# Attention scores in fp32 with one head in each half of the array's rows, in a fused attention and soft-MoE kernel

## The chip, the cores and the metric

One core of one Trainium2 chip runs the whole program. The metric is the device time of one execution in microseconds (us); the time before is the median of three runs, 644.68 us (644.61 to 645.15).

## The reference

Three layers follow each other. Sparse attention over 4 batches and 8 heads, 576 tokens, head size 64:

```python
scores = scale * np.matmul(q, k.transpose(0, 1, 3, 2))
thresh = np.max(scores, axis=-1, keepdims=True) - tau
scores = np.where(scores >= thresh, scores, -1000000000.0)
attn = np.exp(scores - np.max(scores, axis=-1, keepdims=True))
attn = attn / (np.sum(attn, axis=-1, keepdims=True) + 1e-09)
out = np.matmul(attn, v)
```

Then a soft mixture of 8 experts (`d.T @ x` into 32 slots, two layers `w1`, `w2` per expert, and back to 2304 tokens), and a feed-forward layer with weights `w_in` (512 x 2048) and `w_out` with a sigmoid gate. All inputs and outputs are fp32.

## The kernel before

**Stages.** `attention()` runs 16 units; a unit is two heads of one batch. Each unit has nine tiles of 128 query rows by 576 keys: four chunks times two heads (t = 0 to 7), and a tile t = 8 that holds the last 64 rows of both heads. `experts()` follows, then `ffn()`.

**The loop.** In `attention()` one loop (L887) runs over all 144 tiles; iteration i issues `scores(i)` (TensorE), `row_max(i-1)` (VectorE, out of PSUM), `exps(i-1)` (ScalarE), `trans(i-4)` (TensorE transposes of the weights `p`), `mask(i-2)` (VectorE). Product steps `attn_v` (weights times values, tile `o_ps`) run at set offsets of a unit (L932 to L937), and the next unit's q and k are transposed by `prep_rest` and `prep_main` (L939 to L945). From i = 5 the engines keep the order in which the program issues their work (L889); the loads on the queue of SP are not held to it. Scores lie in a pool `ps_s` of two PSUM buffers of two banks each, one buffer for a tile.

**Scores by halves.** `prep_main` transposes q and k of both heads at once; ScalarE copies the result to fp32r (the high half), VectorE takes the difference (the low half, `split`, L328), and DMAs from SP's queue (L397) stack high and low halves of one head on top of each other in `a_st`, `b_st`, `kl0`, `kl1`: 8 moves a unit. With that, one fp32r matmul of 128 rows sums two products, and a tile takes four (L452):

```python
for half in range(2):
    for j, (lh, rh, m) in enumerate(prods):
        te.matmul(ps[0:m, half, 0:HS], lh, rh[:, half * HS:(half + 1) * HS], ...)
```

A tile t = 8 takes eight. `first_unit` (L802) makes the same operands for unit 0 without DMAs, from transposes of each head twice.

**Weights.** Expert weights come in quarters of 0.5 MB into rings. Ring `a` holds 12 quarters; ring `b` takes the place of a pool that frees at i = 126; rings `c` to `k` take freed places near the end of attention (L1002 to L1018). 42 of 64 quarters are held when `experts()` starts; the other 22 are loaded as layer 1 has read `a` and `b` (L1060), and layer 2 `c` and `d` (L1102). SP's queue issues all loads.

Of the kernel before, what the change touches and what calls it, by code (L numbers as in the profile page):

```python
# [19 lines left out]
def kernel(  # L20
# [14 lines left out]
    nc = tc.nc  # L35
# [43 lines left out]
    order = [(1, e) for e in range(4)] + [(2, 0), (2, 1)] + [(1, e) for e in range(4, E)]  # L79
# [28 lines left out]
    def add_ring(name, n, side=LEFT, spread=False):  # L108
        ring_ctx[name] = ctx if name in "bk" else ExitStack()
        rings[name] = ring_ctx[name].enter_context(  # L110
            tc.tile_pool(name="ring_" + name, bufs=1, side=side)
        )
        if n:
            load_quarters(name, n, spread)

# [94 lines left out]
    def late_piece(pool, j, wl):  # L210
        n, kc = divmod(j, KC)
        cols = slice(n * DM, (n + 1) * DM)
        return decoding(
            pool, ("late", j), DM,
            lambda top, rest: po.tensor_add(out=wl[:, kc, cols], in0=top, in1=rest),
        )
# [18 lines left out]
    def attention():  # L235
# [22 lines left out]
        pr = pool(loads, "pr", 1, RIGHT)  # L258
# [7 lines left out]
        b_st = []  # L266
        for i in range(2):
            t = stk[i].tile([P, 2 * R + C * P], F32R, name=f"b_st{i}")
            ve.memset(t[:, 0:R].bitcast(F32), 0.0)
            b_st.append(t)  # L270
# [7 lines left out]
        nat, rest, hl, stacks, vt = {}, {}, {}, {}, {}  # L278
# [40 lines left out]
        def halves(u, nm):  # L319

            if u not in hl:
                hl[u] = {
                    "q": pr.tile([P, 2, S], F32R, tag="q", name="q_hl"),
                    "k": pr.tile([P, 2, S + R], F32R, tag="k", name="k_hl"),
                }
            return hl[u][nm]

        def split(nm, src, hi, lo):  # L328

            if nm == "q":  # L330
                ac.activation(out=hi, in_=src, func=AF.Copy, scale=neg)
                return lambda: ve.scalar_tensor_tensor(
                    out=lo, in0=src, scalar=neg, in1=hi.bitcast(F32),
                    op0=ALU.mult, op1=ALU.subtract,
                )
            ac.copy(out=hi, in_=src)
            return lambda: ve.tensor_sub(out=lo, in0=src, in1=hi.bitcast(F32))

        def prep_rest(u, bank):


# [9 lines left out]
            def after():  # L351
                x = halves(u, "q")
                lows = [split("q", t[:, 0, :], x[:, 0, 0:R], x[:, 1, 0:R])]
                ends = halves(u, "k").rearrange("p a (e n) -> p a e n", n=R)[:, :, 0::S // R, :]
                both = t[:, 1:2, :].to_broadcast([P, 2, R])
                lows.append(split("k", both, ends[:, 0], ends[:, 1]))
                return lambda: [f() for f in lows] and None
# [3 lines left out]
        def prep_main(u, nm, bank):  # L361
# [6 lines left out]
            lo, hi = slice(0, D), slice(D, P)  # L368

            def after():  # L370
                x = halves(u, nm)
                low = split(
                    nm, t.rearrange("p c t -> p (c t)"), x[:, 0, R:S], x[:, 1, R:S]
                )
                return lambda: stack(low)

            def stack(low):
                low()
                x = hl[u][nm].bitcast(F32)
                if nm == "q":  # L380
                    a_st = stk[u % 2].tile([P, S], F32R, tag="a_st", name="a_st")
                    bs = b_st[u % 2]
                    moves = (
                        (a_st[lo, :], x[lo, 0, :]), (a_st[hi, :], x[lo, 1, :]),
                        (bs[hi, R:], x[hi, 0, :]), (bs[lo, R:], x[hi, 1, :]),
                    )
                    stacks[u] = [a_st, bs]
                else:
                    kl0 = stk[u % 2].tile([P, 2, S], F32R, tag="kl0", name="kl0")
                    kl1 = stk[u % 2].tile([P, 2, S + R], F32R, tag="kl1", name="kl1")  # L390
                    moves = [
                        (dst[half], x[src, :, c0:])
                        for dst, src, c0 in ((kl0, lo, R), (kl1, hi, 0)) for half in (lo, hi)
                    ]
                    stacks[u] += [kl0, kl1]
                    hl.pop(u)
                for dst, src in moves:  # L397
                    nc.sync.dma_start(out=dst.bitcast(F32), in_=src)
# [37 lines left out]
        def kl_planes(t):  # L436
            return t[:, 0, :], t[:, 1, :]

        def scores(i):
            u, t = divmod(i, TPU)  # L440
            a_st, bs, kl0, kl1 = stacks[u]
            ps = ps_s.tile([P, 2, 512], F32, tag="s", name="s_ps")


            if t < 2 * C:
                c, h = divmod(t, 2)
                cols = slice((1 + h) * R + c * P, (1 + h) * R + (c + 1) * P)
                prods = [((a_st, bs)[h][:, cols], x[:, 0:S], P) for x in kl_planes((kl0, kl1)[h])]
            else:
                prods = [(bs[:, 0:2 * R], x[:, R:], P) for x in kl_planes(kl1)]  # L450
                prods[1:1] = [(a_st[:, 0:R], x, R) for x in kl_planes(kl0)]
            for half in range(2):  # L452
                for j, (lh, rh, m) in enumerate(prods):
                    te.matmul(
                        ps[0:m, half, 0:HS], lh, rh[:, half * HS:(half + 1) * HS],
                        start=(j == 0), stop=(j == len(prods) - 1),
                    )
            s_ps[i] = ps
# [343 lines left out]
        def first_unit():  # L802


            def both(nm, h):

                if h == 0:
                    t = ps_s.tile([P, 2, 512], F32, tag="s", name="first_t")
                    return t[:, 0, :].rearrange("p (c t) -> p c t", c=C), t[:, 1, 0:R]
                if nm == "q":  # L810
                    return (
                        ps_t.tile([P, C, P], F32, tag="t", name="first_t"),
                        spare(0, [P, R], "first_t"),
                    )
                return bank_m([P, C, P], "first_t"), bank_o([P, R], "first_t")

            wide = {
                nm: stk[0].tile([P, n], F32R, tag=nm, name=nm)
                for nm, n in (("a_st", S), ("kl0", 2 * S), ("kl1", 2 * (S + R)))
            }  # L820
            a_st, kl0, kl1 = wide.values()
            kl0, kl1 = (x.rearrange("p (a n) -> p a n", a=2) for x in (kl0, kl1))
            stacks[0] = [a_st, b_st[0], kl0, kl1]
            k0, l0, k1, l1 = *kl_planes(kl0), *kl_planes(kl1)
            halves = (slice(0, D), slice(D, P))

            def twice(out, rows):
                for half in halves:
                    te.matmul(
                        out[half], rows, ident[0:rows.shape[0], 0:rows.shape[0]],  # L830
                        start=True, stop=True,
                    )

            for nm, h in (("q", 0), ("k", 0), ("q", 1), ("k", 1)):
                main, left = both(nm, h)
                for c in range(C):
                    twice(main[:, c, :], nat[0][nm][:, c, h, :])
                twice(left, rest[0][nm][:, h, :])
                main = main.rearrange("p c t -> p (c t)")
                if nm == "q":  # L840

                    dst = b_st[0][:, R:] if h else a_st
                    low = halves[1 - h]
                    ac.copy(out=dst[:, R:], in_=main)
                    ac.copy(out=dst[:, 0:R], in_=left)
                    for part, src in ((dst[low, R:], main), (dst[low, 0:R], left)):
                        ve.tensor_sub(out=part, in0=src[low, :], in1=part.bitcast(F32))
                else:
                    dst, low, c0 = (k1, l1, R) if h else (k0, l0, 0)
                    ac.copy(out=dst[:, c0:c0 + C * P], in_=main)  # L850
                    ac.copy(out=dst[:, c0 + C * P:c0 + S], in_=left)
                    if h:
                        ac.copy(out=dst[:, 0:R], in_=left)
                    ve.tensor_sub(
                        out=low[:, c0:c0 + C * P], in0=main,
                        in1=dst[:, c0:c0 + C * P].bitcast(F32),
                    )
# [20 lines left out]
        for _ in range(NRA):  # L878
            load_quarters("a", 4, spread=True)
# [518 lines left out]
```

## Time and profile before

| | us |
|---|---|
| median of three runs | 644.68 |
| the profiled execution | 644.8 |
| its span, first to last instruction | 643.0 |
| PE busy / share of the span | 615.1 / 96% |
| DVE busy / share | 428.7 / 67% |
| ACT busy / share | 372.6 / 58% |
| POOL busy / share | 150.9 / 23% |

PE is TensorE, DVE VectorE, ACT ScalarE, POOL GpSimd, SP the engine whose queue issues the DMAs. Ends of matmuls are modelled and overlap, so a stretch of PE is measured from the start of one group to the start of the next. A fp32 matmul shows as two records, a fp32r matmul and a transpose as one. Attention takes the span up to about 360 us, the experts up to about 402, the feed-forward layer the rest.

### The profile page before, as it was taken

What the parts mean: (1) busy time and instruction counts of PE and PEld (TensorE: products, weight loads), DVE (VectorE), ACT (ScalarE), POOL (GpSimd) and SP (SyncE); (2) the same over time, 40 slices, a digit from 0 to 9 for tenths busy, and PEclk for the clock granted to TensorE, in tenths of its full rate; (3) what the DMA queues carried; (4) which work ended last, traced back from release to release, by engine and by line L of the source; (5) the groups of instructions that cost most, each with busy time, mean ns of one, the idle gap of its engine ahead of it and who ended that gap; (6) DMA issues with size and microseconds to landing.
All of it is one profiled execution on the core that took longest, in us unless ns stands there. A gap on an engine that the chain in (4) does not pass through costs nothing.

```text
span 643.0 us, 11172 instructions
## 1 busy us (share of the span) xinstructions
PE 615.1 (96%) x3848; PEld 450.3 (70%) x3848; DVE 428.7 (67%) x1090; ACT 372.6 (58%) x777; POOL 150.9 (23%) x309
## 2 busy tenths in 40 slices
PE   7799999999999999999999899899998999999996
PEld 6667777677776777766776543577776888888884
DVE  5699888898987898978883242999994212242422
ACT  3588777778876787876773010767565353434340
POOL 1263535335352354533441010001100000000000
PEclk9899999999999999999999799999998999999999
DMA  7785676756786577755679899223320000020203
GB/s 198 208 203 127 167 178 182 183 165 161 204 211 172 165 181 183 184 133 156 177 262 333 307 386 378 101 99 131 131 98 1 0 2 0 1 98 1 99 0 98
DMA packets 78568, 97.52 MB, mean 152 GB/s; under 512 B 44592, under 2 KB 48688, under 8 KB 78512
## 3 DMA queue, kind: packets, MB, share of 16 engines
q1 hardware_dynamic: 78512, 96.82, 51.4%
q8 instruction: 30, 0.49, 0.3%
q14 instruction: 26, 0.21, 0.1%
HBM read 64.55 MB, written 4.72 MB: 108 GB/s over the span
## 4 chain that ended last, share of the span: by engine, by line
PE 82%; DMA 6%; DVE 5%; ACT 2%; SPq 2%; issue 1%; ACTq 0%; DVEq 0%
PE s_ps L132 15%; PE o_ps L132 14%; PE y_ps L1289 10%; PE y_ps L1291 10%; PE y_ps L1290 9%; PE pt_ps L132 9%; PE r_ps L132 5%; PE h_ps L1263 2%; DMA w_b<-in_moe_w_dram 2%; DMA raw<-in_moe_w_out_dram 2%; PE acc L1054 2%; PE k_t L132 1%; PE q_t L132 1%; DMA qn<-in_q_dram 1%; DVE p L132 1%
## 5 line engine op out<-in xcount | busy, mean ns | idle before, releaser
L132 ACT ACTIVATE e_sb<-p,mn 128x576 f32<-128x576 f32 x144 | 112.5, 781 | 13.7 <-DVE p L132 12.4
L132 DVE TENSOR_SCALAR_CACHE_REDUCE p<-s_ps 128x576 f32<-128x576 f32 x135 | 101.3, 750 | 26.3 <-PE s_ps L132 19.0
L132 DVE SCALAR_TENSOR_TENSOR p<-p,th,e_sb 128x576 f32<-128x576 f32 x144 | 117.7, 818 | 1.5 <-ACT e_sb L132 1.3
L1289 PE MATMUL y_ps<-wo_h,gh 128*128 128x512 f32 x288 | 114.6, 398 | 0.4 <-ACT gh L1250 0.4
L1290 PE MATMUL y_ps<-wo_l,gh 128*128 128x512 f32 x288 | 113.9, 396 | 0.0
L1291 PE MATMUL y_ps<-wo_h,gw 128*128 128x512 f32 x288 | 113.5, 397 | 0.0
L1252 DVE TENSOR_TENSOR gw<-sg,gh 128x768 fp32r<-128x768 f32 (+2 forms) x49 | 47.0, 962 | 95.1 <-ACT gh L1250 95.1
L132 ACT COPY pt<-pt_ps 128x512 f32<-128x512 f32 x142 | 82.8, 583 | 46.4 <-PE o_ps L132 23.2
L132 POOL TENSOR_TENSOR th<-mn,few 128x1 f32<-128x1 f32 x144 | 64.0, 444 | 180.8 <-DVE p L132 177.5
L1268 ACT ACTIVATE sg<-h_ps 128x512 f32<-128x512 f32 (+1 forms) x96 | 42.4, 489 | 88.3 <-PE h_ps L1263 87.9
L132 PE MATMUL pt_ps<-ident,p 128*128 128x128 f32 x580 | 86.9, 273 | 0.0
L132 PE MATMUL o_ps<-pt,vn 128*64 128x320 f32 (+1 forms) x512 | 85.5, 427 | 0.0
L132 PEld LDWEIGHTS pt_ps<-ident,p 128*128 128x128 f32 x580 | 71.1, 141 | 0.7 <-issue 0.4
L132 PE MATMUL s_ps<-kl,b_st 128*128 128x288 f32 x320 | 68.8, 321 | 1.8 <-DMA kn<-in_k_dram 1.2
L132 PE MATMUL s_ps<-kl,a_st 128*128 128x288 f32 (+1 forms) x320 | 65.7, 318 | 0.7 <-DVE y L132 0.7
L1289 PEld LDWEIGHTS y_ps<-wo_h,gh 128*128 128x128 f32 x288 | 54.3, 189 | 14.3 <-ACT gh L1250 1.1
L132 PEld LDWEIGHTS s_ps<-kl,a_st 128*128 128x128 f32 (+1 forms) x320 | 45.1, 179 | 26.5 <-DVE p L132 9.2
L1291 PEld LDWEIGHTS y_ps<-wo_h,gw 128*128 128x128 f32 x288 | 54.1, 188 | 13.3
L1290 PEld LDWEIGHTS y_ps<-wo_l,gh 128*128 128x128 f32 x288 | 54.3, 189 | 11.4 <-DVE gw L1252 0.2
L132 PEld LDWEIGHTS s_ps<-kl,b_st 128*128 128x128 f32 x320 | 47.8, 191 | 16.5 <-DVE p L132 8.7
L132 PEld LDWEIGHTS o_ps<-pt,vn 128*64 128x64 f32 x512 | 27.3, 135 | 28.3 <-issue 24.7
L1250 ACT CAST gh<-sg 128x768 fp32r<-128x768 f32 (+2 forms) x49 | 40.2, 823 | 1.2
(200 smaller groups left out, 796.3 us busy)
## 6 DMA issues: line engine op xcount, KB each, us to landing
kl<-k_hl SPq DMA_DIRECT2D x30, 320.0 KB, 5.6
kl<-k_hl SPq DMA_DIRECT2D x30, 288.0 KB, 4.2
raw<-in_moe_w_out_dram SPq DMA_DIRECT2D x16, 512.0 KB, 3.3
raw<-in_moe_w_in_dram SPq DMA_DIRECT2D x24, 256.0 KB, 3.4
w_a<-in_moe_w_dram SPq DMA_DIRECT2D x12, 512.0 KB, 4.5
w_a<-in_moe_w_dram SPq DMA_DIRECT2D x6, 1024.0 KB, 10.4
a_st<-q_hl SPq DMA_DIRECT2D x30, 144.0 KB, 2.7
b_st<-q_hl SPq DMA_DIRECT2D x30, 144.0 KB, 2.7
```

What stands on the lines that cost most here:

```text
L132: ins = call(*args, **kw)
L1054: nc.tensor.matmul(acc1[j][kc * NS:(kc + 1) * NS, :], s_in[kc // 2][:, kc % 2, e * NS:(e + 1) * NS], w_rows[1, e, kc][:, j * 512:(j + 1) * ...
L1250: nc.scalar.copy(out=gh[:, a], in_=sg[:, a])
L1252: nc.vector.tensor_sub(out=gw[:, a], in0=sg[:, a], in1=gh[:, a].bitcast(F32))
L1263: nc.tensor.matmul(ps, ws[:, f * P:(f + 1) * P], cs[:, t:t + n, :].rearrange("p t n -> p (t n)"), start=True, stop=True,)
L1268: nc.scalar.activation(out=part, in_=ps, func=AF.Gelu_apprx_sigmoid)
L1289: nc.tensor.matmul(ys[t], gh[:, tk], w_h, start=first, stop=False)
L1290: nc.tensor.matmul(ys[t], gh[:, tk], w_l, start=False, stop=False)
L1291: nc.tensor.matmul(ys[t], gw[:, tk], w_h, start=False, stop=last)
```

## The change

Scores are made from plain fp32 q and k as they come out of the transposes: head 0 in partitions 0 to 63, head 1 in 64 to 127. A matmul contracts over 64 rows of the array; the two heads of a chunk go to two tiles of `ps_s` in turn (both buffers at once), and the tile t = 8 becomes one matmul per head and half, each with its own 64 columns of the array, into one PSUM tile. The splitting, the stacking moves, `b_st` and the pool `pr` go. Scores are issued in even iterations for two tiles, behind `trans`; the product steps and the preparation move to other iterations. A ring `m` holds four quarters from units 10 and 11 on and stays; rings `d` and `e` are halved, and after layer 2 has read it `m` is loaded again; in the feed-forward layer its place holds a partial sum and half of `wl`. The experts are loaded in another order.

```diff
-    order = [(1, e) for e in range(4)] + [(2, 0), (2, 1)] + [(1, e) for e in range(4, E)]
+    order = [(1, 0), (1, 1), (1, 2), (2, 0), (1, 3), (2, 1)] + [(1, e) for e in range(4, E)]
...
             def after():
-                x = halves(u, nm)
-                low = split(
-                    nm, t.rearrange("p c t -> p (c t)"), x[:, 0, R:S], x[:, 1, R:S]
-                )
-                return lambda: stack(low)
...
+                out, src = turned(u, nm)[:, R:S], t.rearrange("p c t -> p (c t)")
                 if nm == "q":
...
+                    ac.activation(out=out, in_=src, func=AF.Copy, scale=neg if u else 1.0)
                 else:
...
-                for dst, src in moves:
-                    nc.sync.dma_start(out=dst.bitcast(F32), in_=src)
+                    ac.copy(out=out, in_=src)
...
             if t < 2 * C:
-                c, h = divmod(t, 2)
-                cols = slice((1 + h) * R + c * P, (1 + h) * R + (c + 1) * P)
-                prods = [((a_st, bs)[h][:, cols], x[:, 0:S], P) for x in kl_planes((kl0, kl1)[h])]
+                both = [ps_s.tile([P, 2, 512], F32, tag="s", name="s_ps") for _ in range(2)]
+                s_ps[i], s_ps[i + 1] = both
+                c0 = R + t // 2 * P
+                prods = [
+                    (both[h], qx[rows, c0:c0 + P], kx[rows, (1 - h) * R:(1 - h) * R + S])
+                    for h, rows in enumerate(heads)
+                ]
             else:
-                prods = [(bs[:, 0:2 * R], x[:, R:], P) for x in kl_planes(kl1)]
-                prods[1:1] = [(a_st[:, 0:R], x, R) for x in kl_planes(kl0)]
+                s_ps[i] = ps_s.tile([P, 2, 512], F32, tag="s", name="s_ps")
+                prods = [(s_ps[i][rows], qx[rows, 0:R], kx[rows, R:]) for rows in heads]
             for half in range(2):
...
+                for ps, lh, rh in prods:
                     te.matmul(
...
+                        ps[:, half, 0:HS], lh, rh[:, half * HS:(half + 1) * HS],
+                        start=True, stop=True, held=True,
                     )
...
         def first_unit():
...
+            for nm, bank in (("q", bank_t), ("k", bank_m)):
+                prep_main(0, nm, bank)()
+            prep_rest(0, bank_s)()
...
+        load_quarters("m", 4, spread=True)
...
-            if i < total:
-                scores(i)
             if 0 <= i - 1 < total:
                 row_max(i - 1)
...
             if i < 4:
                 warm(2)
+            if i < total and (t % 2 == 0):
+                scores(i)
...
-                    else (10, 10, 11, 12, 12, 14, 14, 15, 16, 17 - (x == NU - 2))
+                    else (10, 10, 10, 12, 12, 14, 14, 14, 16, 16)
...
-                if t == (0 if u else 2):
+                if t == 2:
                     s_after = prep_rest(u + 1, bank_s)
-                if t == (0 if u else 3):
+                if t == (2 if u else 3):
                     m_after = prep_main(u + 1, "q", bank_m)
-                if t == (2 if u else 4):
+                if t == (3 if u else 4):
                     m_after = prep_main(u + 1, "k", bank_m)
...
-                swap(even_units, "d", 4)
+                swap(even_units, "d", 2)
...
-                swap(odd_units, "e", 4)
+                swap(odd_units, "e", 2)
...
-                load_quarters("cd"[e], min(4, len(quarters)))
+                load_quarters("mc"[e], min(4, len(quarters)))
...
-        held["wl"] = gp.tile([P, KC, DFF - WA], F32, name="wl", bufs=1)
+        spare_m = rings["m"].tile([P, 4, F1], F32, tag="w", name="part_wl")
```

## Rows read from the trace of the kernel before

**Rows 1.** The page's chain that ended last, by engine, share of the span.

```profile
PE 82%; DMA 6%; DVE 5%; ACT 2%; SPq 2%; issue 1%; ACTq 0%; DVEq 0%
```

**Rows 2.** Busy time by stretch: PE, PEld, DVE, ACT, POOL, clock, DMA share, GB/s.

```profile
49.14:68.56 19.42, 19.42 (x139) 14.31 (x138) 17.47 (x51) 15.68 (x36) 9.13 (x19) 1.00 0.61 150
```

**Rows 3.** The chain in order of time, start and length: left tiles of units 1 and 15.

```profile
49.14 1.24 PE s_ps L132 x8
...
336.57 1.25 PE s_ps L132 x8
```

**Rows 4.** Timeline of PE, one unit: start, length, what, count.

```profile
80.49 0.60 PE L132 MATMUL pt_ps<-ident,p 128*128 128x128 f32 x4
80.93 0.60 PE L132 MATMUL x_ps<-ident,xt 128*128 128x128 f32 x4
...
84.10 0.80 PE L132 MATMUL s_ps<-kl,a_st 128*128 128x288 f32 x4
84.74 0.60 PE L132 MATMUL pt_ps<-ident,p 128*128 128x128 f32 x4
85.27 0.76 PE L132 MATMUL o_ps<-pt,vn 128*64 128x320 f32 x4
...
87.91 0.40 PE L132 MATMUL s_ps<-kl,b_st 128*128 128x288 f32 x1
...
89.06 0.60 PE L132 MATMUL pt_ps<-ident,p 128*128 128x128 f32 x4
...
95.90 0.65 PE L132 MATMUL o_ps<-pt,vn 128*64 128x256 f32 x4
96.48 0.66 PE L132 MATMUL k_t<-ident,kn 128*128 128x128 f32 x4
```

**Rows 5.** Timeline of PE near the end of attention: a long block of products.

```profile
338.84 1.95 PE L132 MATMUL o_ps<-pt,vn 128*64 128x256 f32 x16
340.72 1.20 PE L132 MATMUL pt_ps<-ident,p 128*128 128x128 f32 x9
```

**Rows 6.** Timeline of DVE in the same unit.

```profile
84.94 0.76 DVE L132 TENSOR_SCALAR_CACHE_REDUCE p<-s_ps 128x576 f32<-128x576 f32 x1 [0.44 <-PE s_ps L132]
...
85.62 0.81 DVE L132 SCALAR_TENSOR_TENSOR p<-p,th,e_sb 128x576 f32<-128x576 f32 x1
...
92.35 0.42 DVE L132 SCALAR_TENSOR_TENSOR top<-raw,y 128x256 uint32<-128x256 uint32 x1
92.69 0.81 DVE L132 SCALAR_TENSOR_TENSOR p<-p,th,e_sb 128x576 f32<-128x576 f32 x1
...
93.42 0.28 DVE L132 SCALAR_TENSOR_TENSOR q_hl<-r_ps,few,q_hl 128x64 fp32r<-128x64 f32 x1
...
93.82 0.74 DVE L132 SCALAR_TENSOR_TENSOR q_hl<-q_t,few,q_hl 128x512 fp32r<-128x512 f32 x1
```

**Rows 7.** Timeline of PE at the start; what ended the idle time stands in brackets.

```profile
17.84 0.69 PE L132 MATMUL q_t<-ident,qn 128*128 128x128 f32 x2 [4.07 <-DMA qn<-in_q_dram]
...
28.59 0.40 PE L132 MATMUL s_ps<-kl,b_st 128*128 128x288 f32 x1 [0.41 <-DVE p L132]
...
34.63 0.77 PE L132 MATMUL s_ps<-kl,b_st 128*128 128x288 f32 x4 [1.16 <-DMA kn<-in_k_dram]
```

**Rows 8.** Timeline of SP's queue at the start.

```profile
9.59 0.91 SPq L999 DMA_DIRECT2D w_a<-in_moe_w_dram  x2
10.60 0.65 SPq L296 DMA_DIRECT2D qn<-in_q_dram  x1
...
26.07 3.50 SPq L398 DMA_DIRECT2D kl<-k_hl  x4
29.66 1.40 SPq L296 DMA_DIRECT2D kn<-in_k_dram  x1
```

**Rows 9.** Busy time by stretch, columns as in rows 2: start, and after attention.

```profile
17.80:35.00 17.20, 13.28 (x82) 11.73 (x83) 13.06 (x38) 11.13 (x23) 6.34 (x12) 0.87 0.77 201
...
364.00:368.00 4.00, 4.00 (x28) 1.45 (x24) 0.00 (x0) 0.00 (x0) 0.00 (x0) 0.63 0.63 236
```

More of the change, by code (lines that the diff above doesn't have):

```diff
@@ L114, in add_ring @@
             load_quarters(name, n, spread)
+    add_ring("m", 0)
     def swap(old, name, n):
@@ L214, in late_piece @@
             pool, ("late", j), DM,
-            lambda top, rest: po.tensor_add(out=wl[:, kc, cols], in0=top, in1=rest),
+            lambda top, rest: po.tensor_add(out=wl[kc // 2][:, kc % 2, cols], in0=top, in1=rest),
         )
@@ L265, in attention @@
         ve.memset(v_left, 0.0)
[L266 to L270, printed above, removed]
         xt = tx.tile([P, HP, C * P], F32, name="xt")
@@ L317, in load_v_left, with turned @@
                 )
[L319 to L334, printed above, removed]
-                )
-            ac.copy(out=hi, in_=src)
-            return lambda: ve.tensor_sub(out=lo, in0=src, in1=hi.bitcast(F32))
+        def turned(u, nm):
+            if (u, nm) not in qk:
+                n = S if nm == "q" else S + R
+                qk[u, nm] = stk[u % 2].tile([P, n], F32, tag=nm, name=nm + "x")
+            return qk[u, nm]
         def prep_rest(u, bank):
@@ L351, in after @@
             def after():
[L352 to L357, printed above, removed]
+                ac.activation(out=turned(u, "q")[:, 0:R], in_=t[:, 0, :], func=AF.Copy, scale=neg if u else 1.0)
+                ends = turned(u, "k").rearrange("p (e n) -> p e n", n=R)[:, 0::S // R, :]
+                ac.copy(out=ends, in_=t[:, 1:2, :].to_broadcast([P, 2, R]))
             return after
@@ L434, in weights @@
             return p2[u, t // 2][:, t % 2 * S:(t % 2 + 1) * S]
[L436 to L437 removed]
         def scores(i):
             u, t = divmod(i, TPU)
[L441 to L442 removed]
+            qx, kx = qk[u, "q"], qk[u, "k"]
+            heads = [slice(h * D, (h + 1) * D) for h in range(2)]
             if t < 2 * C:
[L446 to L451 removed]
+                both = [ps_s.tile([P, 2, 512], F32, tag="s", name="s_ps") for _ in range(2)]
[5 more added lines that the diff above has]
+                ]
+            else:
+                s_ps[i] = ps_s.tile([P, 2, 512], F32, tag="s", name="s_ps")
+                prods = [(s_ps[i][rows], qx[rows, 0:R], kx[rows, R:]) for rows in heads]
             for half in range(2):
[L453 removed]
+                for ps, lh, rh in prods:
                     te.matmul(
[L455 to L456 removed]
+                        ps[:, half, 0:HS], lh, rh[:, half * HS:(half + 1) * HS],
+                        start=True, stop=True, held=True,
                     )
[L458 removed]
         def row_max(i):
@@ L802, in first_unit @@
         def first_unit():
[L805 to L857, printed above, removed]
-                    ends = (0, c0 + C * P) if h else (C * P,)
-                    for c1 in ends:
-                        ve.tensor_sub(
-                            out=low[:, c1:c1 + R], in0=left, in1=dst[:, c1:c1 + R].bitcast(F32)
-                        )
@@ L889, in attention @@
             InOrder.on = IN_ORDER and 5 <= i < total
-            if i < total:
-                scores(i)
             if 0 <= i - 1 < total:
                 row_max(i - 1)
-            lows = [f() for f in (t_after, l_after, r_after, s_after, m_after) if f]
+            for f in (t_after, l_after, r_after, s_after, m_after):
+                if f:
+                    f()
             t_after = l_after = m_after = s_after = r_after = None
@@ L914, in attention @@
                 mask(i - 2)
-            for low in lows:
-                if callable(low):
-                    low()
             if o_after:
@@ L1060, in experts @@
                 load_quarters("aaab"[e], 4)
-        for name in ("md", "j", "i", "lg", "h", "g", "f", "e"):
+        for name in ("md", "j", "i", "lg", "h", "g", "f", "e", "d"):
             ring_ctx[name].close()
@@ L1200, in w_at @@
             if c0 >= WA:
-                return held["wl"][:, kc, c0 - WA:c0 - WA + n]
+                return held["wl"][kc // 2][:, kc % 2, c0 - WA:c0 - WA + n]
             return wi[kc // 2][:, kc % 2, c0:c0 + n]
@@ L1232, in experts @@
         list(slots_in(0, P, lambda: pa.tile([P, 512], F32, tag="acc2", name="wq")))
-        for name in "dc":
-            ring_ctx[name].close()
+        ring_ctx["c"].close()
         return ws, cs, wo, stream, decode_next, load_next, slots_in, st.close, held
@@ L1296, in project @@
                             rings["a"].tile([P, GT, DM], F32, tag="wi", name="part", bufs=2) if g < 2
-                            else gp.tile([P, GT, DM], F32, name="part", bufs=1)
+                            else spare_m[:, 0:3, :].rearrange("p a (b n) -> p (a b) n", n=DM)
                         )
@@ L1315, in ffn @@
         leave()
-        held["wl"] = gp.tile([P, KC, DFF - WA], F32, name="wl", bufs=1)
+        spare_m = rings["m"].tile([P, 4, F1], F32, tag="w", name="part_wl")
+        held["wl"] = [
+            spare_m[:, 3, :].rearrange("p (k n) -> p k n", k=2),
+            gp.tile([P, 2, DFF - WA], F32, name="wl", bufs=1),
+        ]
         held["gp"] = gp
```

25 lines of the change are left out of this document (2 added, 23 removed).

## The prediction, made blind

> **What bounds the kernel now.** I read the chain first: 82% of the span is TensorE work and 6% DMA [rows 1]. Then a unit of attention by itself: 19.42 us in which PE is never idle, DVE busy 17.47 [rows 2]. The chain has one left tile per unit; from unit 1 to unit 15 they go from 49.14 to 336.57, 14 units [rows 3]. So attention is bound by the order and length of PE's work; a faster DVE or fewer DMAs help it only where PE waits. PE waits at the start: for q of unit 1 (4.07 us before 17.84), and before 34.63 for a transfer [rows 7]. After attention the expert weights fill the DMA queues.
>
> **Scores, part by part.** Before, a tile costs 84.74 - 84.10 = 0.64 us and a left tile 89.06 - 87.91 = 1.15 [rows 4]; a unit 8 x 0.64 + 1.15 = 6.27. No row shows a fp32 matmul over 64 rows. The nearest rows are the products: fp32, two heads at once, in two halves of the columns. Four records (one step) of 256 columns take 96.48 - 95.90 = 0.58 [rows 4], sixteen take 340.72 - 338.84 = 1.88 [rows 5]. So one round (a record of each head) costs (1.88 - 0.58)/6 = 0.217, and a block of any length 0.58 - 2 x 0.217 = 0.15 on top. In turn the four records alone would need 0.87, so the two column halves do work together. For 288 columns a round is 0.217 x 288/256 = 0.244. A pair of score tiles needs four rounds: 0.98. I take it that row halves overlap as column halves do; if they don't, it is 1.95. To this comes 0.15 for the block, 0.09 to enter it (four transposes take 0.53 ahead of a block, 85.27 - 84.74, and 0.44 ahead of other transposes, 80.93 - 80.49 [rows 4]), and, estimated, 0.05 because a weight load here has 128 columns and not 64, and 0.06 for the transposes that follow a block: 1.32. The 0.05 has the bounds 0 and 0.16 (both heads' loads in turn). Five such blocks a unit (four pairs and the left tile) are 6.60: **+0.33 a unit**.
>
> No row shows two row halves at work. For the overlap there is the Trainium skill, "TensorE: Matmul & The Clock Gate", section "Part 3: Packing small matmuls — row/col tiling": tiles in different row groups run concurrently, four of them 3.07 times as fast as in turn; by an estimate from that figure a pair would be somewhat dearer than the 0.98 above.
>
> **Products.** The same matmuls, but in four blocks and not seven (one block is a stretch of o_ps rows; two of the seven stand in [rows 4]): 3 x (0.15 + 0.09) = **-0.72**. Transposes now follow each, where scores did, and the scores' 0.64 held that loss: 4 x 0.06 = **+0.24**.
>
> **A new wait.** A pair takes both score buffers, so it waits for the row maximum of the last tile before it. Count from the start of a pair: 1.17 to its end, 0.04, row maximum 0.68 (85.62 - 84.94), a decoding step of up to 0.34 (92.69 - 92.35), mask 0.74 (93.42 - 92.69), row maximum 0.76 with its last write, 0.08 to PE: 3.81 [rows 6]. PE's own work from pair to pair, added up from the same prices (transposes 0.11 each): t = 0 to 2, 1.23 + 0.22 + 0.44 + 1.61 + 0.55 + 0.09 = 4.14; t = 2 to 4, 4.57; t = 4 to 6, 5.00; t = 6 to 8, 3.69, where the left tile needs one buffer only. PE is longer in each, so this wait is covered, by 0.33 at the narrowest. From t = 8 to the next unit it isn't: PE has 1.23 + 0.55 + 0.09 = 1.87, the chain 1.17 + 0.04 + 0.76 + 0.08 = 2.05: **+0.18**. Queued behind it on PE are the pair and all later work. The five steps add up to 19.45 against 19.42 measured: the sum of the bold terms, **+0.03 a unit, +0.5 us over 15 units**. Attention as such gains nothing.
>
> **Splitting, stacking, copies.** VectorE loses its low halves, per unit 0.40 + 0.74 for q with the two short ones (93.82 - 93.42, then 0.74) and, estimated as about the same, 0.7 for the 512 columns of k [rows 6]: 1.8 us, off the path. ScalarE makes as many copies as before. Eight moves a unit leave SP's queue and the DMA engines; in the steady part PE never waited for them, so nothing there. The preparation's transposes stay, two iterations later; they are in the sums above. The loads of q and k for unit u + 2 are still issued at t = 5, behind their buffers' release at t = 2 and 3.
>
> **Start.** Here they were on the path. Tile 8 starts at 28.59 and unit 1's second tile at 34.63, after a wait of 1.16 [rows 7] that the profile puts on a load; I put it on the four moves of kl, issued from 26.07 on for 3.50 us in front of that load [rows 8]. From left tile to left tile unit 1 takes 49.14 - 28.59 = 20.55. Unit 0 is worse: q of unit 1 is issued at 10.60 behind two 0.5 MB weight loads [rows 8], and with the idle PE the clock falls (0.87 of full speed in the mean from 17.80 to 35.00 [rows 9], so both levels, 1.2 and 2.4 GHz, are in it). After the change unit 0's operands are two groups of transposes and four copies. If q of unit 1 comes as late as before, pair 4 starts at about 19.7, and half the clock, two chains and a left tile later tile 8 at about 26.8; unit 1 then takes 19.0 (its five steps without one group of transposes): its left tile at 45.8, -3.3. If it comes early enough, pairs follow each other by 3.5 to 3.8 from 9.6 on, tile 8 at 22.7, unit 1's left tile at 41.7, -7.4. The buffer of q is free earlier, as 8 transposes take the place of 40 matmuls, but SP's order is not held, so I take the middle: **-5.5**.
>
> **End of attention, experts, feed-forward.** Ring m brings four quarters early, d and e four fewer: still 42 held, 22 to load. Those 22 start when layer 1 has read ring a, near 366, and the queue had run out of work there (DMA share 0.63 from 364 to 368 [rows 9]); so 1 MB less in flight before that moves nothing: 0. Four more loads of 0.5 MB inside attention lie under PE's work. Layer 2 reads m first and reloads it at the same place as c before: 0. The wait that could open instead is for `wl` in m's place, read out long before: 0.
>
> **Sum.** -5.5 + 0.5 = -5.0. The profiled execution took 644.8, 643.0 of it span; it lies 0.1 above the median. 644.8 - 5.0 = 639.8, against the median 639.7.
>
> **Rivals.** (a) *The left tile's heads in turn.* There both heads write one PSUM tile, in different partitions; the pairs write different tiles. Rows of column halves share a bank and still overlap (0.58, not 0.87 [rows 4]), which speaks against it, but they share their rows of the array. Each left tile would take 0.98 more, 16 of them 15.6: 655.3, slower. It decides once one left tile takes over 1.32 + 0.3. Beside it stands the Trainium skill, "TensorEngine Tiling (Array Packing)", section "Gotcha 1: PSUM Pressure": "Different row tiles cannot access same PSUM bank simultaneously". (b) *No overlap of row halves at all*: 5 x 0.98 x 16 = 78: 718. (c) *The pair's wait*: a mask held up by ScalarE (which has the copies of q and k ahead of an exponential at t = 2 and 3) makes the chain of 3.81 longer than PE's 4.14 to 4.57. Each of three pair steps late by 0.3 would be 0.9 x 15 = 13.5: 653.2, slower. It decides from 0.33 on; DVE's lighter load speaks against it. (d) *The start gains little*: q still late, and the half clock as well as entry costs at the upper bound (0.11 x 5 x 15 = 8.3 at most, of which a third, 2.8): 639.7 + 2.2 + 2.8 = 644.7, no change.
>
> **Chances.** Forecast 0.62, (a) 0.10, (b) 0.06, (c) 0.08, (d) 0.14. A change under 0.2%, 1.3 us, can't be told from none: faster 0.62, same 0.14, slower 0.24. The low end: start at -7.4, no wait at t = 8 and no dearer weight load (0.18 + 0.25, times 15 = 6.5): 631. The high end takes in (a) and (c): 656; (b) is left out.
>
> **What would show it.** Right: left tiles 19.4 to 19.6 apart; two heads' score records starting together, a pair block at about 1.3; unit 1's left tile between 42 and 46; experts as long as before. Wrong: score records of two heads one after the other; a left tile near 2.3; PE idle ahead of pairs at t = 2, 4, 6 and released by DVE; weights landing later after attention.

## The result and the profile after

The changed kernel takes 639.54 us in the median of four runs (637.79 to 640.20), the kernel before 644.64: a ratio of 0.9915, interval 0.9894 to 0.9936. The forecast was 639.7, faster. The profiled execution of after took 639.14, its span 637.3 (643.0 before).

The page of after: its busy times, its mean transfer rate, and its chain that ended last, which answers to [rows 1].

```profile
PE 615.4 (97%) x3778; PEld 417.2 (65%) x3778; DVE 401.1 (63%) x1019; ACT 371.1 (58%) x772; POOL 150.5 (24%) x309
...
DMA packets 67110, 69.97 MB, mean 110 GB/s; under 512 B 42736, under 2 KB 46832, under 8 KB 67056
...
PE 84%; DVE 7%; DMA 4%; ACT 2%; issue 2%; SPq 1%; DVEq 0%; ACTq 0%
```

Before, PE was busy for 615.1 us, DVE for 428.7, and 97.52 MB were moved. So VectorE lost 28 us of work and the DMA engines 28 MB, and TensorE is busy for as long as before. The 5.7 us that the span lost are idle PE: 643.0 - 615.1 = 27.9 before, 637.3 - 615.4 = 21.9 after.

When they went is read from the left tiles of units 1 and 15 in the chain in order of time, which answer to [rows 3]:

```profile
43.85 1.12 PE s_ps L134 x8
...
330.85 1.12 PE s_ps L134 x8
```

Unit 1's is 49.14 - 43.85 = 5.29 earlier than before, unit 15's 336.57 - 330.85 = 5.72; between them lie 287.00 us and not 287.43. The first matmul after attention starts 359.93 - 354.74 = 5.19 earlier, and the span ends 5.7 earlier. So nearly all of the gain is made before 44 us. Units 1 to 15 gave another 0.43, the end of attention behind unit 15's left tile took 0.53 back (23.89 us long, 23.36 before), and the experts and the feed-forward gave 0.5.

Now units 1, 2 and 3 by PE's timeline, which answers to [rows 4]. A pair of tiles is one s_ps row of eight records (64*128); a left tile is one with 64*64.

```profile
45.59 1.67 PE L134 MATMUL s_ps<-kx,qx 64*128 64x288 f32 x8
47.19 0.44 PE L134 MATMUL r_ps<-ident,lw 128*128 128x128 f32 x2
...
50.13 1.24 PE L134 MATMUL s_ps<-kx,qx 64*128 64x288 f32 x8
...
54.69 1.24 PE L134 MATMUL s_ps<-kx,qx 64*128 64x288 f32 x8
...
59.68 1.24 PE L134 MATMUL s_ps<-kx,qx 64*128 64x288 f32 x8
...
63.36 1.19 PE L134 MATMUL s_ps<-kx,qx 64*64 64x288 f32 x8
64.48 0.66 PE L134 MATMUL pt_ps<-ident,p 128*128 128x128 f32 x4
...
65.17 1.57 PE L134 MATMUL s_ps<-kx,qx 64*128 64x288 f32 x8
66.67 0.44 PE L134 MATMUL r_ps<-ident,lw 128*128 128x128 f32 x2
...
84.87 1.48 PE L134 MATMUL s_ps<-kx,qx 64*128 64x288 f32 x8
86.28 0.44 PE L134 MATMUL r_ps<-ident,lw 128*128 128x128 f32 x2
...
93.78 1.24 PE L134 MATMUL s_ps<-kx,qx 64*128 64x288 f32 x8
94.95 0.66 PE L134 MATMUL x_ps<-ident,xt 128*128 128x128 f32 x4
95.56 0.66 PE L134 MATMUL pt_ps<-ident,p 128*128 128x128 f32 x4
```

From start to start (the printed length takes in the tail that overlaps the next instruction), a pair takes 94.95 - 93.78 = 1.17 us, the left tile 64.48 - 63.36 = 1.12. The pair behind the left tile takes longer, by the wait that was forecast: 47.19 - 45.59 = 1.60 in unit 1, 1.50 in unit 2, 1.41 in unit 3, so 0.43, 0.33 and 0.24 of waiting. The steps of unit 1, from pair to pair, to the left tile and to the next pair, are 4.54, 4.56, 4.99, 3.68 and 1.81. In units 2 and 7 the second step is 4.77. In unit 3 alone of the units inside a batch, PE also waits between x's transposes and those behind them (0.61, in the other units 0.49), which makes the third step 5.16 there.

Why the wait differs is on DVE's timeline. In unit 1 the row maximum of the left tile starts behind a mask (from 44.01) and the scaling of the last unit's products (from 44.74), at 45.21; PE had finished that tile at 44.90 (43.78 + 1.12). In unit 3 it starts 0.12 behind PE.

```profile
45.21 0.75 DVE L134 TENSOR_SCALAR_CACHE_REDUCE p<-s_ps 128x576 f32<-128x576 f32 x1
```

A unit's period, by its left tiles, is 19.57 to 19.69 inside a batch (19.42 before). From unit 1 to unit 15, the seven periods around the ends of batches are 1.76 us shorter in all than before, the seven others 1.33 longer: the 0.43. No run takes apart what shortened those around the ends.

The start, by PE's timeline and SP's queue; they answer to [rows 7] and [rows 8].

```profile
6.86 1.09 PE L134 MATMUL q_t<-ident,qn 128*128 128x128 f32 x4 [2.99 <-DMA qn<-in_q_dram]
...
15.94 0.66 PE L134 MATMUL q_t<-ident,qn 128*128 128x128 f32 x4
...
23.88 1.19 PE L134 MATMUL s_ps<-kx,qx 64*64 64x288 f32 x8
```

```profile
9.18 0.65 SPq L292 DMA_DIRECT2D qn<-in_q_dram  x1
...
11.59 1.37 SPq L898 DMA_DIRECT2D w_a<-in_moe_w_dram  x3
```

The load of unit 1's q is issued at 9.18, ahead of the weights of ring a; before, at 10.60 behind two of them. PE takes it up at 15.94 with no wait shown, where it had waited 4.07 us until 17.84. Nobody wrote this order: in both programs the load of unit 1's q stands ahead of those of the weights, and on SP's queue, which isn't held to the program, it came out differently. At its first q the change loses: it transposes both heads at once and so waits 2.99 us for the second load of q, until 6.86, where the kernel before had begun with one head at 3.79. After that idle time four transposes of k take 1.00 us (7.73 to 8.73), where four take 0.49 from 15.94 on. The first scores start at 10.90, not at 9.58. Unit 0's left tile stands at 23.88 instead of 28.59 all the same: 4.71 of the 5.29 are there. Busy time from 15 to 24 us, columns as in [rows 2], after and then before: nearly twice the busy time of PE, at the full clock (2.4 GHz) and not at a mixture with 1.2.

```profile
15.00:24.00 9.00, 8.80 (x60) 6.20 (x60) 8.51 (x24) 7.62 (x15) 2.48 (x8) 1.00 0.99 350
```

```profile
15.00:24.00 9.00, 4.67 (x21) 4.35 (x21) 3.76 (x12) 2.60 (x4) 1.11 (x2) 0.62 0.78 235
```

### The profile page after: what moved, and what is told of

Same layout as the page of the kernel before. It is cut to its first block, busy times and chain, and to the rows that moved or that the text cites. A ratio compares the mean times of both kernels' runs of the same rounds, so it can differ in the third digit from the quotient of the medians.

```text
span 637.3 us, 10662 instructions
## 1 busy us (share of the span) xinstructions
PE 615.4 (97%) x3778; PEld 417.2 (65%) x3778; DVE 401.1 (63%) x1019; ACT 371.1 (58%) x772; POOL 150.5 (24%) x309
## 4 chain that ended last, share of the span: by engine, by line
PE 84%; DVE 7%; DMA 4%; ACT 2%; issue 2%; SPq 1%; DVEq 0%; ACTq 0%
PE s_ps L134 15%; PE o_ps L134 14%; PE pt_ps L134 11%; PE y_ps L1187 9%; PE y_ps L1189 9%; PE y_ps L1188 9%; PE r_ps L134 5%; PE h_ps L1161 2%; DMA w_c<-in_moe_w_dram 2%; PE q_t L134 2%; PE k_t L134 2%; DMA w_a<-in_moe_w_dram 1%; DVE p L134 1%; DVE y L134 1%; PE x_ps L134 1%
## 5 line engine op out<-in xcount | busy, mean ns | idle before, releaser
L134 PE MATMUL s_ps<-kx,qx 64*128 64x288 f32 (+1 forms) x640 | 105.0, 430 | 0.4 <-DVE p L134 0.4
L134 POOL TENSOR_TENSOR th<-mn,few 128x1 f32<-128x1 f32 x144 | 57.7, 401 | 175.8 <-DVE p L134 170.3
L134 PE MATMUL pt_ps<-ident,p 128*128 128x128 f32 x580 | 91.5, 281 | 0.2
L134 PEld LDWEIGHTS pt_ps<-ident,p 128*128 128x128 f32 x580 | 63.7, 141 | 36.1 <-ACT pt L134 10.9
L134 PE MATMUL o_ps<-pt,vn 128*64 128x320 f32 (+1 forms) x512 | 75.8, 418 | 0.0
L134 PEld LDWEIGHTS s_ps<-kx,qx 64*128 64x128 f32 (+1 forms) x640 | 56.5, 177 | 24.8 <-issue 9.0
L134 PEld LDWEIGHTS o_ps<-pt,vn 128*64 128x64 f32 x512 | 31.2, 136 | 30.3 <-issue 16.5
L134 ACT COPY ptr<-r_ps 128x128 f32<-128x128 f32 (+1 forms) x92 | 22.8, 248 | 19.2 <-PE r_ps L134 19.0
L134 ACT ACTIVATE y<-raw 128x256 f32<-128x256 f32 (+1 forms) x44 | 23.9, 543 | 10.9 <-DMA raw<-in_moe_w_out_dram 8.8
```

Source lines behind the costliest of these rows:

```text
L134: ins = call(*args, **kw)
```

## The experiments

My theory: the start gains from the order of the loads and from the moves that are gone; in a steady unit scores, blocks and wait cancel. Rivals: the pairs themselves are the gain; VectorE's lighter load is; the four expert weights held in ring m are. Each run is compared with the kernel before on the same chip.

**The two heads in turn.** All matmuls of one head are queued before the other's.

```diff
-            for half in range(2):
-                for ps, lh, rh in prods:
+            for ps, lh, rh in prods:
+                for half in range(2):
```

> The changed kernel, with the two matmuls of head 0 issued ahead of the two of head 1, instead of head by head for each half. If row halves overlap only where neighbours in the issue order lie in different rows, a pair block goes from 1.18 us to 1.9 to 2.1 (seven or eight rounds of 0.244 instead of four), a unit from 19.6 to 23 or 24, the time to 695 to 715. If TensorE pulls the other head's matmuls ahead by itself, nothing changes: 639.5.

One run gave 637.57. The pair in its timeline of PE, from s_ps to x_ps:

```profile
93.68 1.25 PE L134 MATMUL s_ps<-kx,qx 64*128 64x288 f32 x8
94.86 0.66 PE L134 MATMUL x_ps<-ident,xt 128*128 128x128 f32 x4
```

1.18 us, as in the changed kernel. My view that the two heads have to be neighbours in the queue fell.

**One head's tile at a time.** Each iteration makes one head's tile, in one half of the rows, with nothing in the other half.

```diff
-                both = [ps_s.tile([P, 2, 512], F32, tag="s", name="s_ps") for _ in range(2)]
...
+                s_ps[i] = ps_s.tile([P, 2, 512], F32, tag="s", name="s_ps")
+                c, h = divmod(t, 2)
...
-            if i < total and (t % 2 == 0):
+            if i < total:
```

> The changed kernel with one head's tile per iteration, so that no two row halves ever stand next to each other in the queue. Four rounds of 0.244 and a block's 0.3 for each tile: four blocks a unit more, 4 x 1.28 = 5.1 a unit, 82 in all: 715 to 725. If row halves brought nothing over single heads: 640 to 650.

One run gave 724.22, a unit 24.14. PE's timeline:

```profile
65.83 1.23 PE L134 MATMUL s_ps<-kx,qx 64*128 64x288 f32 x4
66.99 0.44 PE L134 MATMUL r_ps<-ident,lw 128*128 128x128 f32 x2
```

Four records of one head take 66.99 - 65.83 = 1.16, eight of two heads 1.17: the second head is free. That is the overlap of the row halves which the prediction had to borrow from the column halves. Without it attention grows by 24.14 - 19.59 = 4.55 a unit. The Trainium skill, "TensorE: Matmul & The Clock Gate", section "Part 3: Packing small matmuls — row/col tiling", has tiles in different row groups of the array run at the same time; these two rows agree.

**Products in seven blocks again**, at the offsets of the kernel before.

```diff
-                    else (10, 10, 10, 12, 12, 14, 14, 14, 16, 16)
+                    else (10, 10, 11, 12, 12, 14, 14, 15, 16, 17 - (x == NU - 2))
```

> The changed kernel with the product steps at the places of before, so seven blocks of products a unit and not four. The prediction's price is 0.15 + 0.09 + 0.06 = 0.30 for a block: 0.9 a unit, over 15 units 13.5, of which the existing waits at t = 0 and t = 5 can hide a third at most: 648 to 653. If a block's fixed part were only an artefact of how ends of matmuls are modelled: 639.5.

642.10, ratio 0.9975 (0.9953 to 0.9997). Slower than the changed kernel, but by 0.2 to 0.5 a unit inside a batch (19.76 to 20.08), not 0.9. Its timeline of PE says why:

```profile
65.80 1.24 PE L134 MATMUL s_ps<-kx,qx 64*128 64x288 f32 x8
66.97 0.44 PE L134 MATMUL r_ps<-ident,lw 128*128 128x128 f32 x2
...
69.49 1.26 PE L134 MATMUL s_ps<-kx,qx 64*128 64x288 f32 x8
70.68 0.65 PE L134 MATMUL o_ps<-pt,vn 128*64 128x256 f32 x4
71.26 0.27 PE L134 MATMUL r_ps<-ident,qr 64*128 64x64 f32 x1
```

One of the extra blocks stands right behind a pair (0.58 for four records, the price inside a block and no second way in and out). Another fills the time of the wait, and the pair behind the left tile takes 66.97 - 65.80 = 1.17 where it took 1.50 in that unit. So the number of blocks has a price only where transposes stand on both sides and PE isn't about to wait.

**The moves back.** q and k of every unit but the first go to another tile, and from there by eight moves in on-chip memory to where they are read.

```diff
-                ac.activation(out=turned(u, "q")[:, 0:R], in_=t[:, 0, :], func=AF.Copy, scale=neg if u else 1.0)
+                ac.activation(out=staged(u, "q")[:, 0:R], in_=t[:, 0, :], func=AF.Copy, scale=neg if u else 1.0)
...
+                for rows in (slice(0, D), slice(D, P)):
+                    for c in range(2):
+                        cols = slice(c * n, (c + 1) * n)
+                        nc.sync.dma_start(out=dst[rows, cols], in_=src[rows, cols])
```

> The changed kernel with q and k of units 1 to 15 going through eight moves a unit on SP's queue before the scores read them, as before (half the bytes). My theory, that the moves cost at the start alone: unit 1's left tile from 43.8 to 45 to 48, units still 19.6 apart, 641 to 644. The rival, that moves cost all along (queue or traffic): units 0.2 or more longer, 645 or more.

639.02, ratio 0.9927 (0.9909 to 0.9946): what the changed kernel gains. Its moves of unit 1's q and k in SP's queue, and its left tiles of units 0 and 1:

```profile
17.55 2.55 SPq L341 DMA_DIRECT2D qx<-qf  x4
20.20 0.66 SPq L293 DMA_DIRECT2D kn<-in_k_dram  x1
20.96 2.56 SPq L341 DMA_DIRECT2D kx<-kf  x4
```

```profile
23.79 1.19 PE L134 MATMUL s_ps<-kx,qx 64*64 64x288 f32 x8
...
43.69 1.19 PE L134 MATMUL s_ps<-kx,qx 64*64 64x288 f32 x8
```

They stand where the changed kernel's do, with the moves in front of later loads, and the unit is 19.58. Only the last unit is longer, 19.8 instead of 18.41. The moves, each of half the old bytes, cost nothing at the start as such. One thing is not rebuilt: before, the load of unit 2's k stood behind the moves of unit 1's k (26.07 and 29.66 [rows 8]), here it stands ahead of them (20.20 and 20.96). What that order cost isn't measured by itself; the 5.29 leave 0.58 for all of unit 1. So the second cause that I gave for the gain has no run for it, and at most a small part.

**The kernel before with its weights held back.** In the kernel before, the loads of ring a wait behind a GpSimd write into their buffers until unit 4; nothing else is changed.

```diff
-                nc.sync.dma_start(**slow.pop(0))
+                io = slow.pop(0)
+                po.memset(io["out"][:, 0, 0, 0:1], 0.0)
+                nc.sync.dma_start(**io)
```

> The kernel before, with the twelve weight loads of ring a held back to unit 4 on, so that none stands in front of q and k of unit 1. My theory, that these loads are a good part of the start's loss: q of unit 1 lands 3 us earlier, the clock doesn't fall, left tile of unit 0 from 28.6 to 25 to 26, the time 640.5 to 642.5. The rival, that the stacking moves alone hold the start: 644.6.

639.91, ratio 0.9950 (0.9925 to 0.9974). SP's queue, PE's timeline, and the chain in order of time:

```profile
8.48 1.07 SPq L148 DMA_DIRECT2D raw<-in_moe_w_in_dram  x2
9.65 0.65 SPq L296 DMA_DIRECT2D qn<-in_q_dram  x1
```

```profile
14.40 0.44 PE L132 MATMUL q_t<-ident,qn 128*128 128x128 f32 x2 [0.27 <-DMA qn<-in_q_dram]
```

```profile
43.98 1.24 PE s_ps L132 x8
...
331.23 1.25 PE s_ps L132 x8
```

The old scores, splitting, stacking and moves, with a free queue at the start, have unit 1's left tile 49.14 - 43.98 = 5.16 earlier and unit 15's 5.34 earlier. A gain as large as the whole start of the change is had from this alone; its unit is the old 19.42. The load of unit 2's k has moved ahead of the moves here too (20.28 and 21.15).

**Two weight loads ahead of unit 1's q**, in the changed kernel.

```diff
+        for _ in range(NRA):
+            load_quarters("a", 4, spread=True)
+        for _ in range(2):
+            nc.sync.dma_start(**slow.pop(0))
...
-        for _ in range(NRA):
-            load_quarters("a", 4, spread=True)
```

> The changed kernel with two weight loads of ring a issued ahead of unit 1's q and k, which is where SP's queue had them in the kernel before. If the order of loads is the cause of the start's gain, unit 1's left tile goes from 43.8 to 46 to 49 and the time to 642 to 645. If the absent moves are the cause, it stays at 44 and 639.5.

637.64, ratio 0.9904 (0.9883 to 0.9926). Its queue, and PE's first use of that q:

```profile
8.49 1.06 SPq L777 DMA_DIRECT2D w_a<-in_moe_w_dram  x2
9.65 0.66 SPq L292 DMA_DIRECT2D qn<-in_q_dram  x1
```

```profile
15.88 0.66 PE L134 MATMUL q_t<-ident,qn 128*128 128x128 f32 x4
```

Nothing is lost: q is issued 0.47 later and PE takes it up without a wait. So it isn't two loads in front by themselves. The old kernel with late weights has the two loads of raw in front, and there too q comes nearly in time (0.27 of waiting). Before, q was issued at 10.60, with both kinds in front and more of ring a behind. The time from issue to landing of this one load follows the bytes that stand in the queue between the loads of v and it; by the list of DMA issues from 9 to 10.9 us, first here and then in the kernel before:

```profile
qn<-in_q_dram SPq DMA_DIRECT2D x1, 256.0 KB, 5.1
```

```profile
qn<-in_q_dram SPq DMA_DIRECT2D x1, 256.0 KB, 7.2
```

It is 3.4 us in the changed kernel with 0.25 MB of them in front, 4.7 with 0.5 (late weights), 5.1 with 1 MB here, 7.2 with 1.5 MB before. What stands behind q differs as well, so this is no proof; the kernel before with raw held back was not run. And the run here could show a loss only for q later than 15.88, when its PE is ready for it; in the kernel before PE was ready at 17.84 - 4.07 = 13.77. Which loads, together, made PE wait until 17.84 isn't settled; holding back ring a's is enough.

**VectorE's low halves again**, four subtractions a unit, written to a tile that nobody reads.

```diff
+                        return lambda: ve.scalar_tensor_tensor(
+                            out=low, in0=src, scalar=neg, in1=out, op0=ALU.mult, op1=ALU.subtract
+                        )
+                    return lambda: ve.tensor_sub(out=low, in0=src, in1=out)
```

> The changed kernel with VectorE's four subtractions a unit put back, into a tile that nobody reads. VectorE's chain from pair to pair at t = 2 to 4 becomes 3.81 + 1.14 = 4.95 us against PE's 4.57, in the other steps it stays below PE: units up to 0.4 longer, 640 to 646. If VectorE's lighter load were the source of the whole gain, 644.6 or more, with waits in every step; if it counts for nothing, 639.5.

647.49, ratio 1.0052 (1.0031 to 1.0073), slower than the kernel before. PE's timeline in unit 2, and one row of VectorE's:

```profile
76.42 0.63 PE L134 MATMUL k_t<-ident,kn 128*128 128x128 f32 x4 [0.33 <-issue]
...
77.41 1.24 PE L134 MATMUL s_ps<-kx,qx 64*128 64x288 f32 x8
78.71 0.66 PE L134 MATMUL x_ps<-ident,xt 128*128 128x128 f32 x4
```

```profile
75.57 0.74 DVE L134 SCALAR_TENSOR_TENSOR low<-q_t,few,qx 128x512 f32<-128x512 f32 x1
```

A unit is 19.89 to 20.25, and unit 0's left tile comes 1.4 later. The pair behind the left tile doesn't grow (1.48 here, 1.50 in the changed kernel). Two other places do. The pair of t = 4 takes 78.71 - 77.41 = 1.30 instead of 1.17, in unit 1 even 1.46: the wait that was expected. And PE waits 0.33 before the transposes of k, which they didn't before; VectorE reads q's transposes out of PSUM until 76.31, a buffer of the pool that they need too. That it is this buffer I infer from the times. In the kernel before the same work lay off the path. In the changed one it is on the path, so the lighter load of VectorE is no gain in itself, but pairs without it would be a loss.

**Without ring m**, with rings d and e as long as before.

```diff
-            add_ring("m", 0)
...
-        load_quarters("m", 4, spread=True)
...
-                swap(even_units, "d", 2)
+                swap(even_units, "d", 4)
```

> The changed kernel without ring m: rings d and e with four quarters each, the order of experts and the places of wl and of the partial sums as before. My theory, that 42 quarters are held either way and the 22 others start when layer 1 has read ring a: 638.5 to 640.5, and from the first matmul after attention to the slots' first product 42.5 as now. The rival, that early weights shorten the experts: 2 to 3 us slower.

638.64, ratio 0.9923 (0.9897 to 0.9949): the same as with it, left tiles too (23.9, 43.8, 330.7). 42 quarters are held either way, and holding four of them in ring m is worth nothing here.

**Toward a faster version.** First, transposes of the left part brought into the wait behind the left tile, those of x moved behind products, and ten matmuls instead of five ahead of the first q; the first of the two kernels is without the copy of x of one unit, the second, whose diff stands here, has it.

```diff
+            for x, off in started(i):
+                if off == 9 and x < NU - 1:
+                    l_after = across(x, 0)
...
-                    if off == at:
+                    if off == at and (half or last):
...
-                if off == (14 if x == NU - 1 else 22):
+                if off == (14 if x == NU - 1 else 22 if hp == HP - 1 or x == NU - 2 else 23):
```

> The changed kernel with three shifts: the first half's transposes of l ahead of the pair of t = 0 (they fill its wait, 0.24 a unit), the transposes of x one iteration later for three units of four (0.11 waited for ScalarE), and ten instead of five matmuls at the start to bring the clock up before q lands. By the rows of the changed kernel 3.4 + 1.3 + 1 to 1.5: 633 to 635. If the waits only move elsewhere: 639.

> As the first shifted version, but with x of unit 14 at its old place, so that nothing is lost (the first one left out the copy of x of unit 14). By that run's rows, units of 19.37 instead of 19.58 and a first unit 0.5 shorter: 634 to 636.5.

The first: 636.25, ratio 0.9878 (0.9850 to 0.9906). The second, whole: 637.09, 0.9891 (0.9873 to 0.9909), short of the 634 to 636.5 expected. PE's timeline of the second:

```profile
64.25 1.34 PE L134 MATMUL s_ps<-kx,qx 64*128 64x288 f32 x8
65.53 0.66 PE L134 MATMUL pt_ps<-ident,p 128*128 128x128 f32 x4
```

The pair behind unit 2's left tile takes 65.53 - 64.25 = 1.28, where it took 1.50; in unit 3 the wait behind x's transposes is gone too (0.50 instead of 0.61). The unit is 19.37, 0.21 less, and unit 15's left tile is at 327.39, 3.46 earlier than in the changed kernel, of which 0.93 are there at unit 1's: with the ten matmuls PE idles 0.59 and not 2.99 before its first q, and the first scores start at 9.64 and not at 10.90. It is the fastest version here in its marks; by its runs it beats the kernel before, and overlaps the interval of the changed one.

Both that follow build on this version. Second, all products of a half in one block (three blocks a unit), with x's transposes in the stretch that this leaves without products; and third, each unit's products for the left part behind the others, with q's, k's and x's transposes moved. In the third the last product of a unit reads the next unit's left rows of v.

```diff
-                    else (10, 10, 10, 12, 12, 14, 14, 14, 16, 16)
+                    else (10, 10, 10, 10, 10, 14, 14, 14, 16, 16)
```

> The same with all products of a unit's first half in one block (three blocks a unit and not four), and x's transposes at t = 3 to keep PE busy there. By the block's price 0.3 a unit less, by VectorE's chain of 3.5 to 3.8 against PE's 3.9 at t = 2 to 4 hardly a wait: 629 to 633. If the chain is the longer one there: 633 to 636.

```diff
-        steps = [(half, kc) for half in range(2) for kc in ("left", 0, 1, 2, 3)]
+        steps = [(half, kc) for half in range(2) for kc in (0, 1, 2, 3, "left")]
...
-                    else (10, 10, 10, 12, 12, 14, 14, 14, 16, 16)
+                    else (9, 9, 11, 11, 11, 15, 15) + (17 - (x == NU - 2),) * 3
```

> The shifted version with the product steps straight behind a score block (t = 0, 2, 6, 8; v_left's product last in a half), q and k prepared at t = 4 and 5, x at t = 2. A block next to a block costs 0.15 and not 0.30, as the seven-block run showed, and the wait at t = 0 is filled: units 0.4 to 0.6 shorter than 19.37, 626 to 632. If VectorE's chain of 3.5 to 3.8 from pair to pair is then longer than PE's 3.5 (t = 0) and 3.7 (t = 2): 634 to 640.

Both missed widely: 653.24 (ratio 1.0145, 1.0120 to 1.0170) and 654.03 (1.0165, 1.0137 to 1.0193). PE's timelines, three blocks and then the other:

```profile
76.08 0.66 PE L134 MATMUL x_ps<-ident,xt 128*128 128x128 f32 x4 [0.81 <-ACT pt L134]
77.42 0.66 PE L134 MATMUL pt_ps<-ident,p 128*128 128x128 f32 x4 [0.68 <-ACT x_sb L134]
```

```profile
77.96 0.66 PE L134 MATMUL pt_ps<-ident,p 128*128 128x128 f32 x4 [0.79 <-ACT pt L134]
```

In the second, groups of transposes follow each other with no products between them, and each needs a PSUM buffer that ScalarE has to copy out first: 0.81 + 0.68 = 1.49 of the 1.74 us that this unit grew (21.21 for 19.47). The products between them were what gave ScalarE its time. The number of blocks and the new place of x's transposes were not run apart. In the third such waits make up 0.99 us of this unit (0.79 and another 0.20), which is 1.54 longer than in the version it builds on (21.01 for 19.47); the rest isn't explained here.

## Why the prediction was right, point by point

**The total** was right, 639.7 against 639.54, and so was where it comes from. The start was put at -5.5 and came to -5.29 at unit 1's left tile, which was to lie between 41.7 and 45.8 and lies at 43.85.

**The hit of the start was in part luck.** The -5.5 stands between two cases, and neither came about as told. q came early enough for PE, as in the case of -7.4; but the pairs were to start at 9.6 and started at 10.90, behind the wait of 2.99 us for the first q and the slow transposes that follow it, which the prediction didn't reckon. Tile 8 came at 23.88 and not at 22.7, and unit 1 then took 20.0 and not 19.0. The prediction took the middle because "SP's order is not held", and that was right as a doubt: the order that put q first came out of the build.

**Its cause was half right.** The prediction gave q behind the weight loads with the half clock, and the moves of kl in front of a load. For the first there is the old kernel with late weights (-5.16 with nothing else changed), though two weight loads in front of q cost nothing in the changed kernel. The second has no run for it: with moves put back the left tiles stand still. The new count of transposes and copies in unit 0, on which the prediction worked out its two cases, isn't needed for a gain of this size either.

**The score blocks** were right: 1.32 with the way in (0.09) and out (0.06) leaves 1.17 from s_ps to the next row, and 1.17 was measured. The borrowed step, row halves as column halves, is now measured (1.16 for one head, 1.17 for two).

**The unit** came out at +0.16 where +0.03 was forecast. Four of five steps were right, 4.56, 4.99, 3.68 and 1.81 in unit 1 against 4.57, 5.00, 3.69 and 1.87. The step from t = 0 to 2 was mis-sized: 4.54 for 4.14 + 0.18 = 4.32, all of it the wait behind the left tile. The periods around the ends of batches gained 1.76 us, which the prediction didn't reckon, and that gave the 1.33 of the others back: that attention as such came out near nothing is two misses that cancel.

**The price of a block**, 0.15 + 0.09, is right for one alone between transposes and too high beside another block (0.58 in all, without the 0.09 and without a second way out). The sum was not harmed, since the three blocks removed and their transposes were taken together; the expectation of the run with seven blocks, 0.9 a unit, was.

**The wait at t = 8** was forecast as 0.18 and measured as 0.43, 0.33 and 0.24 in units 1, 2 and 3; the other pairs show none (1.17 or 1.18 each, or 1.07 ahead of short transposes). The chain of 2.05 let VectorE take the left tile's row maximum as soon as PE had made it; in unit 1 a mask and the scaling of the last unit's products came first. Of rival (c) this much holds: VectorE is on the path at t = 8, and the four subtractions, put back, cost 0.3 to 0.7 a unit, in part as the wait of the pair of t = 4. The prediction's reason against it, DVE's lighter load, is thus a condition for the forecast.

**Rival (a)** did not come about: the left tile takes 1.12, less than a pair, though its heads share a PSUM tile. The rule of the Trainium skill's page "TensorEngine Tiling (Array Packing)", section "Gotcha 1: PSUM Pressure", that stood beside it isn't borne out for two heads in different partitions of one tile. **Rival (b)**, 718, is what one head at a time gives: 724.22. **Rival (d)** fell with the start.

**Experts and feed-forward** were right at 0: from the first matmul after attention to the end of the span 282.6 us now, 283.1 before, and leaving ring m out changes nothing.

## What to carry to other kernels

Put the change's steady period and its start apart before explaining a gain: here the rewrite of every unit came to nothing, and a start in which weight loads no longer keep PE waiting for unit 1's q gave nearly all of it. The kernel before gets as much by holding those loads back. Where the build may reorder a queue, read its order in the trace; here it changed with lines that the change never touched. Compare a unit with the same unit of the other run: the wait behind the left tile alone goes from 1.41 to 1.60 by unit. Price a matmul that uses part of the array by the block it stands in, by what stands beside it and by whether PE would wait there anyway, not by its records. When an engine off the path gets lighter, ask which new wait that pays for: here the pairs need VectorE's freed time, and taking more blocks out ran into ScalarE's copies.

## What the runs showed of the hardware that I had not expected

- TensorE ran the two row halves together although the queue held all of one head first (1.18 for the pair).
- One head alone in half of the rows costs as much as both (1.16 and 1.17).
- The mean granted clock of a run goes with some of the difference between runs of one kernel, not with all. The version with the filled waits has a span of 630.3 us at a mean clock of 0.995 and 635.3 at 0.987, 0.8% in both. But five runs of the kernel before on one chip, all at 0.987, have spans of 640.1 to 643.0. So differences of a few us between medians say less than the marks inside a trace.
